# When ScalarE makes the hidden-dimension sine tables of an attention and Fourier-mixing kernel

## The chip, the core and the metric

The kernel runs on one core of a Trainium2 chip. A core has a matrix engine (TensorE, PE in the profile, with its weight loads as PEld), a vector engine (VectorE, DVE), an engine for activation functions (ScalarE, ACT), a general engine (GpSimd, POOL) and a queue engine that mainly issues transfers (SyncE, SP). Each engine works through its own list of instructions in order, and semaphores tie the lists together. DMA engines move data between the chip's memory and the core's on-chip memory; here SP and POOL issue the transfers.

The metric is the time of one execution in microseconds (us). All times below are in us unless another unit stands there.

## What is computed

The reference has two parts, in sequence. Eight batches, 12 heads, 448 tokens, 64 columns a head:

```python
q_n = q / (np.linalg.norm(q, axis=-1, keepdims=True) + 1e-06)
k_n = k / (np.linalg.norm(k, axis=-1, keepdims=True) + 1e-06)
scores = np.matmul(q_n, k_n.transpose(0, 1, 3, 2)) / tau
attn = softmax(scores)                       # written out in the reference
x = np.matmul(attn, v)                       # heads side by side: (8, 448, 768)

X = np.fft.fft(np.fft.fft(x, axis=1), axis=2)
u = x + np.real(X)
un = (u - mean(u)) / np.sqrt(var(u) + 1e-06) # over the 768 columns
out = u + np.maximum(un @ w_ch1, 0.0) @ w_ch2
```

`w_ch1` is 768 x 3072 and `w_ch2` is 3072 x 768.

## The kernel before

**A planner.** The kernel doesn't write its instructions out in order. It adds some 3,000 steps, each with a name, the engines that may do it, a cost for each, a priority, the steps that it depends on and the buffers that it takes (`Plan.add`, L131). `Plan.schedule` (L175) then walks through a modelled time: at each point it takes, for the engine that is free first, the ready step of the lowest priority number, and on ScalarE and VectorE it may wait a little for a more urgent one. The result is one fixed list for each engine; semaphore waits follow from the dependences. `SHIFT` (L32) holds corrections to the priorities of single steps, by name and by how often the name has occurred (`"ldt": {0: 665.9}` adds 665.9 to the first step called `ldt`). A step's name ends in its batch: `ex0_1` is of batch 1.

**Dummy products.** `Plan.fill` (L313) puts groups of six 128-column matmuls, whose result nobody reads, into TensorE's list where the planner sees it idle for at least 0.4 us (L1411 and L1412), one group for each 0.4 us (each 0.7 us in the first 14 us). Behind the first W1 product of batch 0 it does so only where the planner's TensorE is busy for less than three quarters of 3.4 us around. All of them have line L1407 in the profile.

**Tables.** The Fourier transform is done with matmuls against cosine and sine tables. Over the tokens these are `CSs` (and `CSn`, its negative), over the 768 columns `CSd` (and `CSp`, the sines before they are negated). VectorE works out the arguments (L517 to L526) into the space of `U` and `UNT`, which is free at that time. ScalarE takes the sines: step `sins` for `CSs` (L552 and L555), step `sind` for `CSd` and `CSp` (L552 and L554). Then `sinp` (L562) writes `CSp` negated into `CSd`, `half` (L566) halves two rows of `CSs`, and `sinn` (L568) makes `CSn`.

ScalarE evaluates from a loaded set of functions. The set with the sine is loaded ahead of all steps (L357); the step `ldt` (L569) loads the set with Ln and Exp once both sine steps are done, and every Ln and Exp stands behind it. Squares and copies are done under either set.

**One batch's attention.** `first_norm` (L607) is for batches 0 and 1. It loads two halves (g = 0 and 1) of K, Q and the last 64 tokens ("T", of Q and K together): `ld_k0_0`, `ld_q0_0`, `ld_t0_0` and so on, from SP (L651). For each part ScalarE squares it (`sqK0_0`, L658) and VectorE sums the squares by row (`ssK0_0`, L660). K's norms are made together, and those of Q and T together: `ln` (L601) and `nrm` (L603) on ScalarE, which give the root, `eps` (L604) and `rcp` (L605) on VectorE. Then three scalings each for K, Q and T (`scK0_0` to `scT2_0`, L685 and L689, on VectorE or GpSimd), transpositions on TensorE (`tk`, `tq`, `tt`, L713 to L738) and copies out (`ek`, `eq` at L704, `et` at L748, the last into `KTD`). Six pairs of heads follow: score products `qk` (L870 to L883), four exponentials `ex` each (L848, three of 900 columns and one of 450), the product with V `pv` (L901, L907), and division by the sum (`rd`, `x`, L925 and L927).

Later batches use `norm` (L751): seven loads into three staging buffers `STG` (L778), squares `sq` (L787), scaling on GpSimd (L796) and transposition by DMA (L802).

**One batch's Fourier part.** Folds `fa`, `f0`, `f1`, `g` on VectorE (L944 to L973) use the symmetry of the tables; `fs` (L989, L994) multiplies with `CSs`, `te` (L1005, L1006) copies out, `fd` (L1032) multiplies with `CSd` and `CSp`, and `u` (L1060) adds x. Statistics `bs`, `ba` (L1089, L1091), `ln2` and `rs` on ScalarE (L1093, L1095), normalisation `un` (L1098), and the transposition into `UNT`: in batch 0 by TensorE (`tn`, L1108, and copies `eu`, L1116), later by DMA (`tru`, L1119).

**The two big products.** `up` (L1151) multiplies with W1 (`h0_b` to `h23_b`, six matmuls each, L1166) and applies the relu (L1182) on ScalarE or VectorE; the second product is at L1197, in batch 0 as `y`, later as seven products of sums and differences (`m1` to `m7`, twelve matmuls each; here called product sets), with outputs `fin` (L1217, L1229) and GpSimd's addition of u (L1222). Batch 0 has one tile of 128 tokens and a pair of tiles; the "first W1 product" is `h0_0` of the single tile, and `h0_1` that of batch 1. The W1 and W2 loads are issued by GpSimd (L582, L583), as are the V loads (L828 to L831); of the W1 loads the first three wait for one V load. Batch 1's q and k loads wait for the first W1 load.

The attention of the next batch runs among the big products of the batch before, so TensorE has both in one list.

Of the kernel before, what the change touches and what calls it, by code (L numbers as in the profile page):

```python
# [12 lines left out]
B, H, S, DH = 8, 12, 448, 64  # L13
DM = H * DH
# [57 lines left out]
}  # L72

# [342 lines left out]
class Kern:  # L416
# [60 lines left out]
    def consts(self):  # L477
        P = self.P
# [8 lines left out]
        cst = self.cst  # L487
# [980 lines left out]
```

## Time and profile before

| | us |
|---|---|
| time, median of 3 runs | 586.5 |
| lowest and highest | 586.41 and 588.08 |
| the profiled execution's own time | 587.25 |
| its span, first to last instruction | 585.4 |

| engine | busy, us | share of the span |
|---|---|---|
| TensorE | 567.2 | 97% |
| VectorE | 420.0 | 72% |
| ScalarE | 350.0 | 60% |
| GpSimd | 205.8 | 35% |

The profile is of one execution. A timeline row gives start, length, engine, line, operation, output and input tiles with their shapes, how many instructions are merged in the row, and in brackets how long the engine was idle before and what ended that. Instructions that follow each other on an engine overlap a little, so a row's length is somewhat more than its share of the engine's time. A row of waits gives who waited, for whom, how long in total, how often, and the longest. Issues and waits of SP's and POOL's queues are not counted as busy time of those engines. "L" numbers are lines of the kernel before.

### The profile page before, as it was taken

How to read it: one execution, taken by the hardware profiler on the slowest of the kernel's cores; microseconds unless marked ns; L12 is line 12 of the kernel's file. 1: busy time of each engine (PE TensorE's matmuls, PEld its weight loads, DVE VectorE, ACT ScalarE, POOL GpSimd, SP SyncE). 2: the span in 40 equal slices, each digit the busy share in tenths (PEclk: the TensorE clock that was granted, in tenths of full speed). 3: DMA queues.
4: the chain of work that ended last, by engine and by line, in shares of the span. 5: the costliest groups of instructions: out<-in, count | busy, mean ns of one | idle time of the engine just before them, and what ended most of it. 6: DMA issues, size and time to landing. Idle time of an engine off the chain costs nothing.

```text
span 585.4 us, 15046 instructions
## 1 busy us (share of the span) xinstructions
PE 567.2 (97%) x6160; PEld 441.4 (75%) x6160; DVE 420.0 (72%) x980; ACT 350.0 (60%) x672; POOL 205.8 (35%) x316
## 2 busy tenths in 40 slices
PE   3889999999999999999999999999999999999997
PEld 3678887677687776978687688778688688778684
DVE  7879888888688668886778767957777757832222
ACT  7785896259864587548856785356746565224140
POOL 8434424440372524632460346341551200200302
PEclk9999999999999999999999999999999999999999
DMA  9999999972394735944299259472179210130101
GB/s 208 197 231 170 166 182 123 173 168 59 69 165 84 162 70 100 173 105 83 65 141 142 55 149 90 118 166 57 28 127 72 49 49 1 54 82 1 41 16 54
DMA packets 187637, 62.12 MB, mean 106 GB/s; under 512 B 166704, under 2 KB 185392, under 8 KB 187568
## 3 DMA queue, kind: packets, MB, share of 16 engines
q1 hardware_dynamic: 129648, 38.35, 33.8%
q0 software_dynamic: 57920, 22.81, 31.2%
q8 instruction: 48, 0.79, 0.5%
q14 instruction: 21, 0.17, 0.1%
HBM read 51.90 MB, written 11.01 MB: 107 GB/s over the span
## 4 chain that ended last, share of the span: by engine, by line
PE 85%; DMA 5%; DVE 4%; ACT 4%; POOL 1%; issue 1%; SPq 0%; POOLq 0%; DVEq 0%; ACTq 0%
PE PS L1166 34%; PE PS L1197 34%; PE PS L907 5%; PE PS L870 5%; DMA W2b<-in_moe_w_ch_dram 3%; DMA STG<-in_k_dram 2%; PE PS L994 2%; PE PS L901 2%; PE PS L1032 2%; ACT E L848 1%; PE PS L882 1%; PE PS L883 1%; ACT HQ L658 1%; DVE SM L660 0%; DVE ACG L944 0%
## 5 line engine op out<-in xcount | busy, mean ns | idle before, releaser
L1166 PE MATMUL PS<-UNT,W1b 128*128 128x256 bf16 (+1 forms) x2304 | 233.4, 259 | 0.3 <-DVE SM L604 0.3
L1166 PEld LDWEIGHTS PS<-UNT,W1b 128*128 128x128 bf16 x2304 | 199.0, 98 | 23.5 <-issue 2.8
L848 ACT ACTIVATE E<-PS 128x900 bf16<-128x900 f32 (+1 forms) x192 | 147.8, 829 | 28.3 <-PE PS L870 26.0
L1197 PE MATMUL PS<-W2b,HQ 128*128 128x384 bf16 x768 | 134.0, 326 | 0.0
L1182 ACT ACTIVATE HQ<-PS 128x512 bf16<-128x512 f32 x120 | 71.6, 597 | 97.2 <-PE PS L1166 96.6
L796 POOL TENSOR_TENSOR QH<-STG,SM 128x256 bf16<-128x256 f32 x126 | 77.5, 641 | 98.9 <-DVE SM L605 81.1
L1197 PEld LDWEIGHTS PS<-W2b,HQ 128*128 128x128 bf16 x768 | 73.4, 98 | 45.8 <-issue 1.7
L1292 DVE TENSOR_TENSOR HQ<-HQ 128x512 bf16<-128x512 bf16 x141 | 62.6, 460 | 44.5 <-ACT HQ L1182 26.7
L1222 POOL TENSOR_TENSOR OUTB<-OUTB,U 128x192 f32<-128x192 f32 x66 | 38.5, 603 | 147.0 <-ACT OUTB L1217 146.3
L1197 PE MATMUL PS<-TX,HQ 128*128 128x384 bf16 x396 | 71.6, 326 | 0.0
L1197 PEld LDWEIGHTS PS<-TX,HQ 128*128 128x128 bf16 x396 | 37.5, 98 | 23.8 <-issue 1.1
L907 PE MATMUL PS<-VB,E 128*128 128x65 bf16 x1152 | 51.0, 193 | 0.0
L787 ACT ACTIVATE QH<-STG 128x384 f32<-128x384 f32 x84 | 42.4, 521 | 11.7 <-DMA QT<-QH 4.1
L1182 DVE TENSOR_SCALAR HQ<-PS 128x512 bf16<-128x512 f32 x42 | 29.0, 692 | 27.8 <-PE PS L1166 27.7
L907 PEld LDWEIGHTS PS<-VB,E 128*128 128x128 bf16 x1152 | 47.5, 97 | 1.4
L789 DVE TENSOR_REDUCE SM<-QH 128x6 f32<-128x384 f32 x84 | 44.1, 537 | 4.8 <-ACT QH L787 4.6
L901 PE MATMUL PS<-VZ,E 128*128 128x130 bf16 x192 | 41.7, 220 | 0.4 <-ACT E L848 0.4
L1251 POOL DMA_INDIRECT out_dram<-OUTB,IDX x20 | 21.3, 1064 | 57.4 <-DVE OUTB L1229 26.8
L870 PE MATMUL PS<-QT,KT 64*128 64x225 bf16 x576 | 39.1, 259 | 1.1 <-ACT E L848 0.7
L1060 DVE TENSOR_TENSOR U<-ACG,X 128x384 bf16<-128x384 f32 (+3 forms) x70 | 38.3, 575 | 0.8
L1229 DVE TENSOR_TENSOR OUTB<-PS,OUTB 128x384 f32<-128x384 f32 x33 | 18.3, 556 | 23.2 <-PE PS L1197 22.5
L870 PEld LDWEIGHTS PS<-QT,KT 64*128 64x128 bf16 x576 | 22.7, 94 | 15.5 <-issue 5.7
(132 smaller groups left out, 623.6 us busy)
## 6 DMA issues: line engine op xcount, KB each, us to landing
STG<-in_q_dram SPq DMA_DIRECT2D x18, 384.0 KB, 3.9
STG<-in_k_dram SPq DMA_DIRECT2D x18, 384.0 KB, 4.3
VB<-in_v_dram POOLq DMA_DIRECT2D x24, 192.0 KB, 6.7
W1b<-in_moe_w_ch_dram POOLq DMA_DIRECT2D x12, 384.0 KB, 7.2
W2b<-in_moe_w_ch_dram POOLq DMA_DIRECT2D x12, 384.0 KB, 7.6
out_dram<-OUTB SPq DMA_DIRECT2D x7, 384.0 KB
TX<-in_k_dram SPq DMA_DIRECT2D x2, 576.0 KB, 5.8
TX<-in_q_dram SPq DMA_DIRECT2D x2, 576.0 KB, 6.8
```

The lines of the kernel that those rows point to most:

```text
L787: P.add("act", lambda a, sq=sq, src=buf[:, w * x:w * x + w]: a.activation(sq, src, ACTF.Square), t_act(w), pr, f"sq{i}_{b}", reads=bn, wri ...
L789: P.add("dve", lambda v, o=SS[:, i, H // ns * x:H // ns * (x + 1)], sq=sq: v.tensor_reduce(o, sq.rearrange("p (h d) -> p h d", d=DH), AX.X ...
L796: r = v.tensor_tensor(v3(qh)[:, h:h + 4], v3(buf)[:, h:h + 4], RN[:, i, h:h + 4].unsqueeze(2).to_broadcast((128, 4, DH)), AluOp.mult)
L848: return a.activation(o, self.PS[:, bk:bk + nc_, 0:SQ2], ACTF.Exp, scale=1.0 / self.tau)
L870: i = pe.matmul(self.PS[:, bk + h, c0:c0 + NK], self.KT[r, jj, kt * 128:(kt + 1) * 128], self.QT[r, jj, cols], start=True, stop=True)
L901: r = pe.matmul(o, st(6), self.VZ[:, j, :], start=not split, stop=(split and i == 0), skip_group_check=True)
L907: r = pe.matmul(o[:, 65 * h:65 * h + 65], st(2 * kt + h), self.VB[:, kt, 2 * j + h, :], start=(split and i == h == kt == 0), stop=((not sp ...
L1166: r = pe.matmul(self.PS[:, bk, x * n:(x + 1) * n], self.W1b[:, j, ft * 128:(ft + 1) * 128], self.UNT[:, j, cs], start=(j == 0), stop=(j == ...
L1182: return e.activation(o, i, ACTF.Relu) if e is self.nc.scalar else e.tensor_relu(o, i)
L1197: r = pe.matmul(self.PS[:, bk, 0:n], lhs(f), rhs(f), start=(start and f == 0), stop=(stop and f == NF // 2 - 1), skip_group_check=True)
L1222: r = g.tensor_tensor(self.OUTB[:, ob, xs], self.OUTB[:, ob, xs], self.U[:, ut, xs], AluOp.add)
L1292: P.add("dve", lambda v: v.tensor_tensor(cs(o), cs(a), cs(bq), op), 0.46, -0.5, f"{nm}{k}_{b}", reads=rd, writes=hr(o)(k))
```

## The change

Only `CSs` and its sines are made at the start. The load of the Ln and Exp set, now step `ldt0`, stands behind `sins` alone, and batch 0's norms wait for that load. A second load of the sine set (`ldt1`) stands behind all exponentials of batch 0 (`self.exps`); `sind` follows it, and then a load of the Ln and Exp set again (`ldt`), behind which the Ln and Exp steps of batch 1 and of the layer normalisation stand. So ScalarE loads a set four times in all instead of two. `sind` has priority 10 instead of -5.

All corrections in `SHIFT` are replaced; with them the planner gives all five engines other lists.

```diff
 SHIFT = {
-    "iota": {0: -285.2}, "tps": {1: -362.7}, "ktd0": {0: 43.6}, "ix0": {0: -4.2}, "vz1": {1: 15.9}, "half": {0: 121.6}, "ld_k0_0": {0: -761.2},
...
+    "iota": {0: -840.7}, "cst": {0: -19.8}, "tqd": {0: -145.4}, "tps": {0: -28.6, 1: -75}, "vz0": {0: 9.3}, "vz1": {0: 285.2}, "ldt0": {0:
+    230.9}, "sinp": {0: 10.8}, "ldt": {0: 665.9}, "ld_q0_0": {0: 1.8}, "ld_t0_0": {0: 1.8}, "rcp0": {0: -210.2, 1: -210.2}, "sqQ0_0": {0:
...
         def tables():
-            done = [table(sd, self.CSd, DM, -5, "d", [], "CSd")]
-            done.append(table(ss, self.CSs, S, -5, "s", [], "CSs"))
+            ld0 = P.add("act", lambda a: a.preload_act_table_set("natural_log_exp_and_others"), 1.3, -5, "ldt0",
+                        order=[table(ss, self.CSs, S, -5, "s", [], "CSs")])
+            self.trig = trig = P.add("act", lambda a: a.preload_act_table_set("trig_and_small"), 1.3, 10, "ldt1", order=[ld0])
+            done = [table(sd, self.CSd, DM, 10, "d", [trig], "CSd")]
+            self.ldt0 = ld0
...
-            self.ldt = P.add("act", lambda a: a.preload_act_table_set("natural_log_exp_and_others"), 1.3, -5, "ldt", order=done)
+            self.ldt = P.add("act", lambda a: a.preload_act_table_set("natural_log_exp_and_others"), 1.3, 10, "ldt", order=done)
...
         P.add("act", lambda a: a.activation(SS, SS, ACTF.Ln, bias=self.cst[:, 0:1]),
-              0.28, pr, f"ln{b}", reads=ssn + ["cst"], writes=ssn, order=[self.ldt])
+              0.28, pr, f"ln{b}", reads=ssn + ["cst"], writes=ssn, order=[self.ldt if b else self.ldt0])
...
         self.attn(0)
+        self.trig.order += tuple(self.exps)
         for b in range(self.nb):
```

81 rows, old and new, of the table SHIFT are left out of this document.

## The prediction

> **What bounds the kernel now.** I read the page's span, then busy time by stretches cut where the first W1 product of batch 0 starts (53.91), where the first W2 product starts (94.64), and where the last product ends (582.3), and then TensorE's longest wait behind 53.95. In a row of stretches stand its length, then TensorE's busy time, weight loads, VectorE, ScalarE and GpSimd, the granted clock, DMA.
>
> ```profile
> span 585.4 us, 15046 instructions
> ```
> ```profile
> 0.00:53.91 53.91, 40.04 (x587) 32.31 (x588) 45.49 (x102) 40.70 (x67) 28.04 (x53) 1.00 1.27 202
> 53.91:94.64 40.73, 39.59 (x569) 34.12 (x570) 35.14 (x78) 31.79 (x58) 13.21 (x18) 1.00 1.16 170
> 94.64:582.30 487.66, 487.57 (x5006) 374.97 (x5003) 338.81 (x800) 277.47 (x548) 164.54 (x245) 1.00 0.55 90
> 582.30:585.40 3.10, 0.00 (x0) 0.00 (x0) 0.56 (x1) 0.00 (x0) 0.00 (x0) 1.00 0.47 190
> ```
> ```profile
> PE PS L882 <- ACT E L848: 0.8, 1, 0.8
> ```
>
> From 94.64 to 582.30 TensorE is busy 487.57 of 487.66 us at full clock. Between 53.91 and 94.64 it is idle 40.73 - 39.59 = 1.14 us, 0.8 of it the wait of the third fence, for ScalarE. So the span is four terms: the start of the first W1 product (53.91), the matmul work behind it (39.59 + 487.57 = 527.16), the idle time behind it (1.14 + 0.09 = 1.23), and the tail (3.10). They give 585.4. A change in the first 54 us counts only by how far it moves that first product, and each matmul added behind it counts in full.
>
> **The start: what is removed and moved.** ScalarE works alone through a chain there.
>
> ```profile
> 6.37 1.15 ACT L658 ACTIVATE E<-TX 128x1152 f32<-128x1152 f32 x1
> 7.84 0.93 ACT L552 ACTIVATE CS<-UNT,MV 128x770 bf16<-128x770 f32 x1
> 8.67 0.83 ACT L554 ACTIVATE TX<-U 128x770 bf16<-128x770 f32 x1
> 9.51 1.28 ACT L569 ACT_TABLE_LOAD   x1
> 10.81 0.31 ACT L601 ACTIVATE SM<-SM,MV 128x18 f32<-128x18 f32 x1
> 12.74 1.15 ACT L658 ACTIVATE E<-TX 128x1152 f32<-128x1152 f32 x1
> 15.65 0.22 ACT L603 ACTIVATE SM<-SM 128x24 f32<-128x24 f32 x1
> 19.83 2.17 ACT L848 ACTIVATE E<-PS 128x900 bf16<-128x900 f32 x3
> ```
> ```profile
> TX<-in_q_dram SPq DMA_DIRECT2D x2, 576.0 KB, 6.8
> ...
> UNT<-F SPq DMA_TRANSPOSE x25, 2.8
> ```
>
> The square of the first K (6.37) ends at 7.52 in both. Then stood a small square, the two sines that move (7.84 to 9.50) and the table load. In the order built for the changed kernel the load follows at once (7.5 to 8.8), then the square of Q (to 9.9, here it starts at 12.74; its load is now the second that SP issues, at about 1.3, and with 6.8 to landing it is there at 8.1), K's Ln (0.2), the small square (0.4), K's Exp (0.2), a square of the second half (1.05), Q's Ln, a small square, Q's Exp: 12.65. Here that Exp ends at 15.87, so Q's norms come 3.2 us earlier.
>
> VectorE then has more in its way, as it scales K in between:
>
> ```profile
> 11.99 1.50 DVE L689 TENSOR_TENSOR QH<-TX,SM 128x384 bf16<-128x384 f32 x3
> 16.53 0.49 DVE L685 TENSOR_TENSOR TX<-TX,SM 128x128 bf16<-128x128 f32 x2
> 16.94 1.49 DVE L689 TENSOR_TENSOR TX<-TX,SM 128x384 bf16<-128x384 f32 x3
> ```
>
> Its third K scaling (0.5), a reciprocal (0.25), two Q scalings (0.95) and one of the tail (0.25) put the inputs of the first Q transposition at about 15.1, against 17.5 here (16.94 plus one of three): 2.4 us. One of two KTD copies leaves ScalarE, 0.35. I put the first exponential of batch 0 at 17.05, **2.8 us earlier** than 19.83.
>
> ```profile
> 29.27 1.46 ACT L848 ACTIVATE E<-PS 128x900 bf16<-128x900 f32 x2 [0.84 <-PE PS L870]
> 31.21 9.18 ACT L848 ACTIVATE E<-PS 128x900 bf16<-128x900 f32 x12 [0.48 <-PE PS L870]
> 40.27 1.17 ACT L658 ACTIVATE OUTB<-W2b 128x1152 f32<-128x1152 f32 x1
> ```
>
> The 24 exponentials take 20.5 us here, up to the square at 40.27. Twelve take 9.18, so 24 take 18.4, with four small norms some 19.2; the rest is waits (0.84 + 0.48 in these rows) for the second half's scaled rows. Those rows now stand ahead of need by the same kind of count (second-half K scaled from 20.5, last Q at 26, wanted at 26.8). I leave 0.3 of waiting: last exponential at 17.05 + 19.2 + 0.3 = 36.55, **3.8 earlier** (bounds: 2.8 if all waits stay, 4.6 if the rest goes too).
>
> **From the last exponential to the first W1 product.** Here 40.35 to 53.91, 13.55 us.
>
> ```profile
> 41.47 1.35 DVE L660 TENSOR_REDUCE SM<-OUTB 128x18 f32<-128x1152 f32 x1
> 46.81 0.54 ACT L1005 ACTIVATE E<-PS 65x450 bf16<-65x450 f32 x1 [1.38 <-PE PS L994]
> 48.81 1.01 DVE L1060 TENSOR_TENSOR U<-PS,X 128x384 bf16<-128x384 f32 x2
> 49.85 1.02 DVE L1089 BATCH_NORM_STATS2 ACG<-U 128x6 f32<-128x384 bf16 x2
> 53.91 7.53 PE L1166 MATMUL PS<-UNT,W1b 128*128 128x128 bf16 x132 [0.29 <-DVE SM L604]
> ```
>
> ScalarE now gets a load (1.28), the two sines (1.66), and batch 1's square (1.05) first: 4.0 us after the last exponential. VectorE no longer puts the reduction at 41.47 (1.35) ahead of the fold, so the second fold product can run at +4.2; its copy-out ends at +5.8 where it now ends at +7.0 (46.81 + 0.54). The load and the sines hide under fold and product; without that cover they would cost 2.94. That 1.2 us is then given back: VectorE now does five u additions ahead of the statistics instead of two (3 x 0.5), and two K scalings of batch 1 (0.95) ahead of the normalisation. Meanwhile ScalarE does the second table load and two squares and is done at +9.9, before the variance's Ln can start (+10.6). Summed: first W1 product at +13.5, the same. So it starts at **50.05, 3.85 earlier**.
>
> A rule speaks against this change: the Trainium skill (ScalarE: Activation LUTs, What ACT_TABLE_LOAD costs) gives a switch 1.28 us plus a drain of about 1.38, and says to do all of one set before switching. The row at 9.51 shows 1.28, and Ln follows at 10.81, 0.02 behind it; no drain is seen, and the sum goes by the row.
>
> **The negated copies go to GpSimd.** The CSs one (900 columns) stood on VectorE; now it is on GpSimd ahead of the V loads, and the CSd one (770) behind the eighth W1 load.
>
> ```profile
> 5.69 0.74 POOL L530 MEMSET KTD<- 128x768 bf16 x1
> 8.30 0.78 POOL L566 TENSOR_SCALAR CS<-CS 1x225 bf16<-1x225 bf16 x1
> 9.86 3.35 POOL L828 DMA_DIRECT2D VB<-in_v_dram  x3 [0.32 <-POOL IDX L540]
> ```
>
> Not shown by this trace: bounds are 0.74/768 = 0.97 ns a column (0.9 us for 900) and 0.78/225 = 3.5 ns (3.1 us). I take 1.5, nearer the memset, as that row has the same 128 lanes. Starting near 8.9, it lets the V loads go at 10.5 instead of 9.86 (12.1 by the upper bound). SP's loads keep the DMA engines busy to about 13, so I count 0, and 1 at the most. The second lies between +2.9 and at most +5.6, before the product that reads it (+5.9): 0.
>
> **Behind the first W1 product.** The real matmuls are the same. What differs are the groups of six dummy matmuls (L1407): the built order has 11 of them behind the first W1 product, not 2. One stands in batch 1's attention, two before batch 1's first W1 product, eight at the end of batch 1's products. Two of them are seen here:
>
> ```profile
> 186.16 4.06 PE L1197 MATMUL PS<-TX,HQ 128*128 128x384 bf16 x24
> 190.06 4.06 PE L1197 MATMUL PS<-W2b,HQ 128*128 128x384 bf16 x24
> ...
> 256.35 0.83 PE L1407 MATMUL PS<-W1b 128*128 128x128 bf16 x12
> 257.02 1.14 PE L1166 MATMUL PS<-UNT,W1b 128*128 128x256 bf16 x9
> ```
>
> Twelve take 257.02 - 256.35 = 0.67, so a group takes 0.335, and nine more take **3.0 us**. They are nothing only where TensorE would wait anyway, and at the eight it would: the next W1 product's last input is now normalised on VectorE behind an output addition that follows the sixth of seven product sets. A set of twelve takes half of 190.06 - 186.16, 1.95, so six end at 11.7; two VectorE steps of 0.5, a transposition of 2.8 from issue to landing (the page's median for UNT) and a little issue time make some 16, against 13.65 for the seven sets. With the groups TensorE gets there at 16.9 (13.65 + 2.7 and a score product of 0.5), so the time is lost either way and no wait adds to it.
>
> **Idle behind it.** Batch 0's second and third tiles are now transposed after 11 and 15 of the 24 W1 groups; by VectorE's order (0.5 each) their inputs come 0.4 and 0.6 late. Then batch 1's attention, between its first and its last score product:
>
> ```profile
> 64.28:93.78 29.50, 28.48 (x393) 23.35 (x390) 24.46 (x54) 25.34 (x44) 6.69 (x10) 1.00 1.12 176
> ```
> ```profile
> 75.80 0.83 PE L1166 MATMUL PS<-UNT,W1b 128*128 128x256 bf16 x6
> 76.47 0.49 PE L725 MATMUL PS<-TX 128*128 128x128 bf16 x3
> 87.33 0.52 ACT L787 ACTIVATE QH<-STG 128x384 f32<-128x384 f32 x1
> ```
>
> In the built order 19 W1 groups lie in this stretch, not 23. A group takes 76.47 - 75.80 = 0.67, so TensorE has 28.48 - 2.7 = 25.8 to do. ScalarE's four squares of batch 2 (0.52 less overlap, some 1.8; one of them is behind the 0.8 wait) now stand behind the exponentials, copies and output steps about cancel: 25.34 - 1.8 = 23.5. With 3 of this run's 4.2 idle kept it needs 26.5, so TensorE waits 0.7. I take 0.4 + 0.6 + 0.7 and 0.2 more, 1.9, against 1.23 (bounds 0.4 and 4.7).
>
> **Sum**, against the profiled execution: 50.05 + 527.16 + 3.0 + 1.9 + 3.1 = 585.2 of span, 0.2 less than 585.4. That run took 587.25 in all; the median of the runs is 586.5. I carry the difference over: 586.5 - 0.2 = **586.3**.
>
> **Rivals.** (1) *The start's gain survives.* The exponentials lose all waits (first W1 product at 49.3) and the idle time behind is 0.4: 49.3 + 527.16 + 3.0 + 0.4 + 3.1 = 583.0, so 584.1. For: TensorE has only 1.14 idle in that stage now, 0.8 of it for the squares that move. Against: two tile transpositions placed early.
>
> (2) *ScalarE becomes the bound in batch 1's attention.* If its chain keeps the 29.50 us of this run, the four W1 groups that no longer lie between are missed: TensorE waits 29.5 - 25.8 = 3.7, with the two tiles 4.7: 585.2 + 2.8 = 588.0 of span, so 589.1. It decides from the point where ScalarE's chain is longer than 25.8. For: 23.5 of work in 25.8 is 91%, against 86% now. Against: 1.2 of its idle time was the wait for the load of batch 2, which goes.
>
> (3) *Each switch costs twice its row.* If ScalarE lost as much again as a load takes (1.28), the copy-out would slip by 1.1 and the second load would push the variance's Ln 0.75 further: 586.3 + 1.9 = 588.2. Against it stands the 0.02 between load and Ln. The drain of the Trainium skill's section above is this mechanism, and the trace so far speaks against it.
>
> (4) *The change doesn't bring the exponentials forward*, because Q's load lands late: 3.0 + 0.7 more than before, 590.2. Q's 6.8 to landing speaks against.
>
> **How the numbers follow.** A measurement tells 0.3%, 1.8 us, from no change. Forecast 0.47 (585.2 to 587.8 by itself), rival 1 0.24, rival 2 0.21, rival 3 0.04, rival 4 0.04. Faster is rival 1: 0.24. Slower (above 588.3) is rival 2, rival 4 and a part of 3: 0.27. The same is the rest: 0.49. The range goes from 583.5 (rival 1 with the bound of 4.6 on the exponentials) to 589.2 (rival 2).
>
> **What would show it.** First exponential near 17, last near 36.5, first W1 product near 50; both new table loads at 1.28 with the next instruction at once; nine more dummy groups at 0.335 each and no wait beside the last eight. Wrong if the first W1 product is later than 51.5, or if TensorE idles over 3 us behind its first W1 product.

## The result and the profile after

The changed kernel takes 591.02 us, the median of its runs, against 587.33 us for the kernel before beside it; the ratio is 1.0051, with a 95% interval from 1.0034 to 1.0067. It is slower by 0.5%. One of its 20 runs took 1497.18 us, and the ratio leaves it out. The forecast was no change, 586.3 us, and its range ended at 589.2. The profiled execution took 592.52 us in all, 1.5 us more than the median, so its span shows the loss somewhat large.

The page's span, and busy time by stretches of the changed kernel: up to the first W1 product of batch 0 (53.67), up to the first W2 product (96.59), up to the end of the last product (587.00), and the tail. The columns are those of the rows of before.

```profile
span 590.7 us, 15088 instructions
```
```profile
0.00:53.67 53.67, 39.10 (x552) 31.27 (x553) 44.52 (x102) 43.81 (x69) 29.68 (x51) 0.97 1.20 194
53.67:96.59 42.92, 42.92 (x613) 37.91 (x612) 34.53 (x76) 33.17 (x61) 14.97 (x20) 0.96 1.27 169
96.59:587.00 490.41, 488.99 (x5018) 375.96 (x5015) 338.20 (x793) 277.99 (x555) 166.07 (x246) 1.00 0.53 89
587.00:590.70 3.70, 0.00 (x0) 0.00 (x0) 0.56 (x1) 0.00 (x0) 0.40 (x1) 0.83 0.40 159
```

The start, which was to gain 3.85 us, gained 0.24 (53.67 for 53.91). Behind it TensorE is busy 42.92 + 488.99 = 531.91 us and idle 0.00 + 1.42 us. New is the granted clock of 0.97 and 0.96 in the first two rows: before it was 1.00 there. The longest waits of TensorE from 40 us on:

```profile
PE PS L1118 <- DVE F L1108: 2.6, 1, 2.6
PE PS L1176 <- DMA UNT<-F: 0.4, 1, 0.4
PE PS L880 <- DMA KT<-QH: 0.4, 1, 0.4
```

L1118 is the transposition of batch 0's first tile (`tn0_0`), L1108 the tile's normalisation on VectorE (`un0_0`). To see what that waited for, first VectorE's timeline there, then ScalarE's, from its last table load on:

```profile
47.27 0.17 DVE L1101 BATCH_NORM_AGGREGATE MV<-ACG 128x2 f32<-128x12 f32 x1
47.39 1.03 DVE L699 TENSOR_TENSOR QH<-W2b,SM 128x384 bf16<-128x384 f32 x2
50.72 0.67 DVE L1108 TENSOR_SCALAR F<-U,MV 128x768 bf16<-128x768 bf16 x1 [2.31 <-ACT MV L1105]
```
```profile
43.04 1.28 ACT L579 ACT_TABLE_LOAD   x1
44.34 0.31 ACT L611 ACTIVATE SM<-SM,MV 128x18 f32<-128x18 f32 x1
44.92 1.16 ACT L668 ACTIVATE OUTB<-W2b 128x1152 f32<-128x1152 f32 x1 [0.28 <-DVE U L1070]
45.99 0.20 ACT L613 ACTIVATE SM<-SM 128x18 f32<-128x18 f32 x1
49.03 1.16 ACT L668 ACTIVATE W2b<-W2b 128x1152 f32<-128x1152 f32 x1 [2.84 <-DMA W2b<-in_q_dram]
50.10 0.28 ACT L1103 ACTIVATE MV<-MV 128x1 f32<-128x1 f32 x1
50.41 0.20 ACT L1105 ACTIVATE MV<-MV 128x1 f32<-128x1 f32 x1
```

The variance was there at 47.27 + 0.17 = 47.44. Its Ln (L1103) was free to start then, but it stands on ScalarE behind the square of batch 1's first Q half (L668, `sqQ0_1`), and that waited 2.84 us for its load. The load is now the last of the six that SP issues for batch 1; before it was the fourth. It alone, issued at 31.26, in the view of DMA issues (last number: us from issue to landing):

```profile
W2b<-in_q_dram SPq DMA_DIRECT2D x1, 576.0 KB, 17.7
```

So it landed near 49.0, and nothing that the tile needs was in it. While TensorE had no work, its clock fell. Stretches from the last K transposition to the late tile (48.81 to 51.45), to the first W1 product, to the return of the clock (56.96), and on:

```profile
48.81:51.45 2.64, 0.00 (x1) 0.00 (x1) 0.73 (x2) 2.31 (x5) 0.82 (x1) 0.75 1.19 156
51.45:53.67 2.22, 2.22 (x22) 2.22 (x23) 2.12 (x5) 1.25 (x3) 0.82 (x1) 0.50 1.13 139
53.67:56.96 3.29, 3.29 (x33) 3.29 (x32) 2.33 (x6) 0.49 (x1) 0.85 (x2) 0.50 1.36 172
56.96:96.59 39.63, 39.63 (x583) 34.62 (x581) 32.20 (x70) 32.68 (x61) 14.12 (x19) 1.00 1.26 169
```

The clock column (third from the right) is 0.75 in the first row, as the fall comes about half way through it, and then 0.50 until 56.96. The 3.29 us of W1 products in the third row would have taken half as long, so 1.65 us are lost behind the first W1 product, and some more ahead of it. Against the forecast's sum:

| term, us | forecast | profile after |
|---|---|---|
| start of the first W1 product | 50.05 | 53.67 |
| matmul work behind it, dummy groups included | 527.16 + 3.0 | 531.91, of it 1.65 by the halved clock |
| idle behind it | 1.9 | 1.42 |
| tail | 3.1 | 3.70 |
| span | 585.2 | 590.7 |

### The profile page after: what moved, and what is told of

Its sections match the earlier page's. It is cut to its first block, busy times and chain, and to the rows that moved or that the text cites. A ratio compares the mean times of both kernels' runs of the same rounds, so it can differ in the third digit from the quotient of the medians.

```text
span 590.7 us, 15088 instructions
## 1 busy us (share of the span) xinstructions
PE 571.0 (97%) x6178; PEld 445.1 (75%) x6178; DVE 417.8 (71%) x970; ACT 355.0 (60%) x684; POOL 211.1 (36%) x316
## 4 chain that ended last, share of the span: by engine, by line
PE 88%; DMA 5%; POOL 2%; issue 1%; SPq 1%; DVE 1%; ACT 0%; POOLq 0%; DVEq 0%
PE PS L1176 37%; PE PS L1207 33%; PE PS L917 5%; PE PS L880 5%; DMA W2b<-in_q_dram 3%; PE PS L1004 2%; PE PS L911 2%; PE PS L1042 2%; DMA W1b<-in_moe_w_ch_dram 1%; SPq L661 1%; DMA KT<-QH 1%; PE PS L892 1%; PE PS L893 1%; POOL VB L838 1%; PE PS L1418 0%
## 5 line engine op out<-in xcount | busy, mean ns | idle before, releaser
L1176 PE MATMUL PS<-UNT,W1b 128*128 128x256 bf16 (+1 forms) x2304 | 237.3, 260 | 0.4 <-DMA UNT<-F 0.4
L1192 ACT ACTIVATE HQ<-PS 128x512 bf16<-128x512 f32 x122 | 72.8, 597 | 91.0 <-PE PS L1176 89.6
L806 POOL TENSOR_TENSOR QH<-STG,SM 128x256 bf16<-128x256 f32 x126 | 80.5, 664 | 95.4 <-DVE SM L615 81.9
L1207 PE MATMUL PS<-TX,HQ 128*128 128x384 bf16 x396 | 70.4, 326 | 0.0
L1192 DVE TENSOR_SCALAR HQ<-PS 128x512 bf16<-128x512 f32 x40 | 27.6, 691 | 25.9 <-PE PS L1176 25.5
L1227 ACT ACTIVATE OUTB<-PS 128x384 f32<-128x384 f32 x33 | 16.2, 492 | 34.5 <-PE PS L1207 34.3
```

The costliest lines, as they stand in the source:

```text
L806: r = v.tensor_tensor(v3(qh)[:, h:h + 4], v3(buf)[:, h:h + 4], RN[:, i, h:h + 4].unsqueeze(2).to_broadcast((128, 4, DH)), AluOp.mult)
L1176: r = pe.matmul(self.PS[:, bk, x * n:(x + 1) * n], self.W1b[:, j, ft * 128:(ft + 1) * 128], self.UNT[:, j, cs], start=(j == 0), stop=(j == ...
L1192: return e.activation(o, i, ACTF.Relu) if e is self.nc.scalar else e.tensor_relu(o, i)
L1207: r = pe.matmul(self.PS[:, bk, 0:n], lhs(f), rhs(f), start=(start and f == 0), stop=(stop and f == NF // 2 - 1), skip_group_check=True)
```

## The experiments

All act on the planner's finished lists, so nothing else changes its place. `move(engine, step, behind)` takes a step out of an engine's list and puts it behind another (a last number says behind which of several of that name), `hold` puts dummy groups ahead of a TensorE step and `drop` takes some out ahead of one. With these helpers, line numbers are up to 19 higher than in the changed kernel. "First W1" is the first W1 product in the profile; ratios are to the kernel before, run beside each.

| version | first W1 | span | median of runs | ratio, 95% interval |
|---|---|---|---|---|
| the changed kernel | 53.67 | 590.7 | 591.02 | 1.0051 (1.0034 to 1.0067) |
| Q square behind | 50.00 | 584.5 | 587.39 | 0.9996 (0.9977 to 1.0014) |
| wait filled with dummy groups | 52.77 | 586.9 | 588.94 | 1.0028 (1.0013 to 1.0042) |
| changed kernel, no groups behind the first W1 | 55.65 | 593.7 | 592.32 | 1.0076 (1.0054 to 1.0098) |
| Q square behind, no groups behind | 52.97 | 589.3 | 591.16 | 1.0061 (1.0044 to 1.0078) |
| two loads behind the Q load | 50.96 | 586.3 | 588.21 | 1.0011 (0.9997 to 1.0025) |
| Q load second | 51.14 | 585.3 | 589.64 | 1.0034 (1.0016 to 1.0052) |
| both squares behind | 50.15 | 584.6 | 587.58 | 1.0002 (0.9989 to 1.0014) |
| both squares behind, deferral undone | 52.31 | 587.1 | 589.23 | 1.0027 (1.0017 to 1.0037) |
| both behind, earlier tile, four groups | 50.18 | 584.3 | 586.37 | 0.9975 (0.9961 to 0.9989) |
| both behind, earlier tile, all groups | 50.53 | 588.2 | 589.48 | 1.0032 (1.0016 to 1.0048) |
| both behind, four groups | 50.27 | 588.3 | 589.30 | 1.0029 (1.0009 to 1.0048) |
| both behind, earlier tile, four groups, copy-out first | 50.12 | 583.9 | 585.66 | 0.9969 (0.9954 to 0.9983) |
| negated copy behind the V loads | 50.89 | 586.2 | 588.25 | 1.0005 (0.9982 to 1.0028) |

**The square's place.** First the square alone is moved:

```diff
+        self.P.move("act", "sqQ0_1", "ek2_1")
         self.P.emit(self.nc, self.es)
```

> The changed kernel; only the square of batch 1's first Q half (sqQ0_1) moves on ScalarE, from ahead of the variance's Ln of batch 0's first tile to behind the copies of that tile and the third K copy. Theory (ScalarE waits there 2.84 us for the load that lands at 49.01, with the Ln behind it): Ln starts near 47.5 instead of 50.10, the first W1 product near 51.0 instead of 53.67, TensorE's 2.64 us wait ahead of the transposition shrinks below 0.8, its clock stays at 1.00, so the W1 groups behind take 0.335 and not 0.65 each: some 4 us less than the changed kernel's profiled span of 590.7, 586 to 587. Rival (VectorE's five u additions, or the table switches, hold the tile back anyway): first W1 product still past 53, span within 1 us of the changed kernel's.

ScalarE's timeline of that version:

```profile
45.27 0.20 ACT L619 ACTIVATE SM<-SM 128x18 f32<-128x18 f32 x1
47.13 0.29 ACT L1109 ACTIVATE MV<-MV 128x1 f32<-128x1 f32 x1 [1.66 <-DVE MV L1107]
...
50.20 1.18 ACT L674 ACTIVATE W2b<-W2b 128x1152 f32<-128x1152 f32 x1
```

The Ln now waits for the variance alone and starts at 47.13; the first W1 product starts at 50.00, where the forecast had put it (50.05). The clock stayed at 1.00. The span fell by 6.2 us, more than expected, and the runs from 1.0051 to 0.9996. The rival falls. This profiled execution took 586.30 us, 1.1 less than the median, and the changed kernel's 1.5 more than its own, so the spans show more of a gain than the runs.

**A second square in the same place.** The second K half's square (`sqK1_1`) also stands ahead of the Ln. In the version with the Q square behind and no groups, which has the same order ahead of the first W1 product, its load was late instead. ScalarE's rows there:

```profile
45.06 0.31 ACT L617 ACTIVATE SM<-SM,MV 128x18 f32<-128x18 f32 x1
47.49 1.16 ACT L674 ACTIVATE OUTB<-W2b 128x1152 f32<-128x1152 f32 x1 [2.12 <-DVE ACG L1105]
48.56 0.20 ACT L619 ACTIVATE SM<-SM 128x18 f32<-128x18 f32 x1
49.72 0.29 ACT L1109 ACTIVATE MV<-MV 128x1 f32<-128x1 f32 x1 [0.95 <-DVE MV L1107]
```

The wait of 2.12 us is put down to VectorE's statistics (L1105), which this square does not read; its load landed at 47.42 by the trace. The Exp behind it (48.56) holds up a step of the norms on VectorE that stands ahead of the tile's second statistics, so the variance comes late. So both squares were moved, and in two other versions the loads:

```diff
+        self.P.move("act", "sqQ0_1", "ek2_1")
+        self.P.move("act", "sqK1_1", "ek2_1")
```

> The changed kernel; on ScalarE both squares of batch 1's late loads (second K half, first Q half) move behind the copies of batch 0's first tile and the third K copy. Theory: nothing ahead of the variance's Ln depends on a load that lands after 43; first W1 product at 49.5 to 50.3 in every run, clock 1.00, span 583.5 to 585, and the median of the runs about 1 us under that of the version with one square moved, as the K square's wait (2.1 us in one profile) goes too. Rival (the squares are needed soon, and their reductions or the second half's norms then hold batch 1's attention back): waits of 1 us or more on TensorE between 60 and 90.

First W1 product at 50.15, span 584.6, clock 1.00, and no wait of TensorE over 0.4 us behind it. But the median, 587.58, is not under that with one square moved (587.39), so the runs show no gain from the second move.

```diff
+        self.P.move("sp", "ld_q1_1", "ld_q0_1")
+        self.P.move("sp", "ld_t1_1", "ld_q1_1")
```

> The changed kernel; on SyncE alone, batch 1's loads of the second Q half and the second tail (ld_q1_1, ld_t1_1) move behind the load of the first Q half, which so goes from sixth to fourth and the second K half from fifth to third. ScalarE's order is that of the changed kernel. Theory (the Ln waits behind squares for loads): both squares find their data, landed by 41 or so; no wait over 0.8 us on ScalarE ahead of the variance's Ln, first W1 product near 50.0, clock 1.00, span 583.5 to 585.5. Rival (it is the square's place, or the work on VectorE, whatever the load): first W1 product past 52.

With ScalarE's order untouched and the two needed loads earlier, no square waited: Ln at 48.09, first W1 product at 50.96, 2.7 earlier than in the changed kernel. That is later than the 50.0 expected, and the span of 586.3 is 0.8 above what was expected; by ScalarE's timeline the fold product's copy-out, ahead of both squares, ended 0.6 later here (43.24 for 42.61). So the load's lateness is the cause of the wait, not the work around it.

```diff
+        self.P.move("sp", "ld_q0_1", "ld_k0_1")
```

> The changed kernel; on SyncE alone the load of batch 1's first Q half moves from sixth to second, so that the second K half is the last to land (47 to 49 by the landings seen). Theory: the square of that K half, which stands ahead of the Q square on ScalarE, waits in its place, 2 to 4 us, the Ln starts no earlier than 49.3, first W1 product past 52, no gain of over 1.5 us on the changed kernel's profiled span of 590.7. Rival (only the Q load matters): first W1 product near 50, span near 584.5.

Here the theory missed in the profile: the K half's load, now last, had landed by 45.09, when its square was due at 45.36, and the first W1 product started at 51.14. The runs spread from 586.4 to 591.9 us, six of the twelve with a mean granted clock under 0.999, and the median is 589.64. That is as if the wait came in some executions and not in others, but those have no trace, so this run settles nothing.

**The halved clock.** Eight groups of six dummy matmuls are put ahead of `tn0_0`, where TensorE waited:

```diff
+        self.P.hold("tn0_0", 8, self.id_op, warm(self.ID))
```

> The changed kernel with eight more dummy groups on TensorE between the second K transposition of batch 1 and the transposition of batch 0's first tile, where it waited 2.64 us; ScalarE's order is untouched. Theory (the wait itself costs, and beside it the clock that falls to half behind it): ScalarE still waits 2.8 us, the first W1 product starts near 53.3, but the granted clock stays 1.00 and the first W1 groups take 0.335: 1.7 to 2.2 us less than the changed kernel's profiled run. Rival (the clock falls for another reason, as more power drawn by other engines, or is tied to the changed start): clock still 0.5 from about 50 to 57.

ScalarE's row of the waiting square, and TensorE's stretch from 50.20 to 56.80, where the changed kernel had a clock of 0.50:

```profile
47.72 1.16 ACT L687 ACTIVATE W2b<-W2b 128x1152 f32<-128x1152 f32 x1 [1.90 <-DMA W2b<-in_q_dram]
```
```profile
50.20:56.80 6.60, 6.47 (x116) 6.30 (x114) 5.63 (x13) 3.22 (x9) 1.91 (x3) 1.00 1.32 172
```

The square still waited (1.90; the load landed 1.3 earlier than in the changed kernel's profile), and the clock stayed at 1.00. This profile alone doesn't show that the groups kept it there. The tile's normalisation on VectorE and TensorE's rows:

```profile
49.41 0.48 DVE L1127 TENSOR_SCALAR F<-U,MV 128x768 bf16<-128x768 bf16 x1 [1.01 <-ACT MV L1124]
```
```profile
48.63 2.84 PE L1437 MATMUL PS<-TX 128*128 128x128 bf16 x48
51.31 0.50 PE L1137 MATMUL PS<-TX,F 128*128 128x128 bf16 x6
```

The tile was there at 49.89, so without the groups TensorE would have waited some 1.2 us by an estimate (its K transpositions end at 48.79), and a wait of that size can leave the clock at 1.00 (see the versions with the earlier tile below). The eight groups ended only near 51.3, so here they held the product back by 1.4 us; the gain in span, 3.8 for the 1.7 to 2.2 expected, has the earlier landing in it. The runs are better evidence: the mean clock is under 0.999 in one of the 11 with groups, and in ten of the 19 without. And with the Q square behind, it is so in none of the 12 runs that have the groups behind the first W1 product, and in all six of the version without those. So the idle time brings the clock down. In the runs the ratio fell from 1.0051 to 1.0028, and without the wait to 1.0002: some 1.35 us for what the groups saved and 1.5 us for what they didn't, of 587, with intervals about as wide.

**What the deferral is worth.** Both squares moved, and the second sines made at the start again, without the two extra loads:

```diff
+        self.P.order["act"] = [x for x in self.P.order["act"] if x.name not in ("ldt1", "ldt")]
+        self.P.move("act", "sind", "sqK0_0")
```

> As the version with both squares moved, but the second pair of sine tables is made at the start again, ahead of the first of the table loads, and the two other table loads are gone: the deferral is undone, the new priorities stay. Theory as in the prediction (the two switches and the two sines hide behind the last exponential, and at the start they stand in the chain): first exponential 2.1 us later (near 18.4), first W1 product 1.7 to 2.1 us later than with both squares moved, span as much longer. Rival (the deferral only moves the 2.94 us from one end of the chain to the other): first W1 product within 0.5 us.

ScalarE's timeline at the start of this version:

```profile
7.19 0.94 ACT L565 ACTIVATE CS<-UNT,MV 128x770 bf16<-128x770 f32 x1 [0.42 <-DVE UNT L539]
8.04 0.83 ACT L567 ACTIVATE TX<-U 128x770 bf16<-128x770 f32 x1
8.88 1.28 ACT L573 ACT_TABLE_LOAD   x1
...
18.94 0.91 ACT L864 ACTIVATE E<-PS 128x900 bf16<-128x900 f32 x1
```

The first exponential starts at 18.94, against 16.41 with the deferral, and the first W1 product at 52.31 against 50.15; the runs go from 1.0002 to 1.0027. Of 2.53 us at the start 2.16 arrive at the first W1 product, so with these lists the deferral is a gain. The lists were planned with it, though: the kernel before, planned without it, is level with the version with both squares moved (1.0002). What the two switches cost in the end isn't separated here.

**Why the load is late.** GpSimd's timeline of the changed kernel shows the negated copy (L578) ahead of the first V load:

```profile
8.17 2.48 POOL L578 TENSOR_SCALAR HQ<-CS 128x900 bf16<-128x900 bf16 x1
10.72 0.14 POOL L546 IOTA IDX<- 64x8 int32 x1
11.53 1.27 POOL L838 DMA_DIRECT2D VB<-in_v_dram  x1 [0.67 <-POOL IDX L546]
```

```diff
+        self.P.move("pool", "sinn", "ld_v3_0")
```

> The changed kernel; on GpSimd alone the negated copy of 900 columns (2.48 us there in its profile) moves from ahead of batch 0's V loads to behind them, ahead of the W1 loads. Theory (both count: the Q load is last in SyncE's queue, and everything behind the V loads lands later because that copy held them back): the first V load is issued 1.7 us or more earlier than 11.53, the first W1 load lands 1.5 us or more earlier than 24.46, the Q load lands at 46 to 47.5 instead of 49.01, ScalarE's wait shrinks from 2.84 to 0.3 to 1.5 us, the first W1 product starts at 51 to 52.5 and the span is 586 to 588.5. Rival (the order of SyncE's loads alone sets the landing): landing past 48.5, wait over 2.3 us.

The V load went at 8.76, but the copy now stands ahead of the W1 loads, and the first of these landed at 24.77, no earlier than 24.46. The Q load landed at 47.17, the wait was 1.20, first W1 product 50.89 (51 to 52.5 expected), ratio 1.0005. The landing and the wait came as the theory had them, one of its steps did not. And with the same order of loads, the Q load landed between 46.1 and 51.5 in the profiles of twelve of the versions, so this one landing proves little.

That the place in SP's queue counts is shown by the version with the loads reordered, where the Q load was fourth again and landed at 43.49. But in the kernel before, also fourth, it landed at 37.96, 12.3 behind its issue and not 16.0. So the place is not all. The traces show a difference at GpSimd's W1 loads. In the kernel before, the fifth to seventh are issued at 27.74, 31.43 and 32.29, all behind the Q load (25.69). In the changed kernel the fourth to sixth are issued at 26.24, 27.11 and 28.82, all ahead of it (31.26), and none of them had landed by then. Whether these hold the Q load back, no run tests; what GpSimd adds stays open.

**The dummy groups.** The second `fill` is left out:

```diff
-        self.P.fill(first, self.est - 20.0, self.id_op, warm(self.W1b[:, 0, 0:128]), 0.75)
```

> The changed kernel without any dummy group behind the first W1 product (11 fewer: 1 in batch 1's stretch, 2 ahead of batch 1's first W1 product, 8 at the end of its products). Theory as in the prediction (the first three cost 0.335 each, the last eight stand where TensorE waits for a transposition anyway): 1.0 us less, and TensorE idles 2 to 3 us ahead of batch 2's first W1 product; if that idle time halves the clock as the one at 49 did, up to 1.7 us is lost again. Rival (each group costs its 0.335): 3.7 us less and no new wait. The wait at 48.8 to 51.5 stays as it is.

> Both edits together: the square behind the copies and no dummy group behind the first W1 product. Theory: the two gains add, 4 + 1 = 5 us less than the changed kernel's profiled span (585 to 586), so level with or just under the kernel before. Rival (the groups cost their full 3.7): 582 to 583.5, clearly faster than the kernel before.

TensorE's longest waits of the version with the Q square behind and no groups, and the stretches around the first W1 product of batch 2 (199.11):

```profile
PE PS L1182 <- DVE U L1076: 2.3, 1, 2.3
PE PS L886 <- DMA QT<-QH: 1.3, 1, 1.3
```
```profile
195.00:199.20 4.20, 0.65 (x9) 0.45 (x10) 4.10 (x12) 2.69 (x7) 1.53 (x3) 0.94 0.89 207
199.20:203.00 3.80, 3.80 (x23) 2.79 (x23) 1.06 (x3) 1.24 (x4) 2.04 (x3) 0.61 1.11 196
```

Where eight groups stood, TensorE now waits 1.3 + 2.3 us, and the clock falls to half behind it. Without groups neither version is faster than with them (1.0076 for 1.0051, and 1.0061 for 0.9996, six runs each). So those groups stand in a wait, as forecast, and the wait belongs to the new order: batch 2's second tile (`un1_2`) is normalised behind two output additions. Four more versions test that, all with both squares behind. (a) moves this tile ahead, with the Ln of the first tile, the transposition and a score product; (b) drops seven of the eleven groups (the last three lines).

```diff
+        self.P.move("act", "rs0_2", "sq0_4", 0)
+        self.P.move("act", "ln20_2", "sq0_4", 0)
+        self.P.move("sp", "tru1_2", "tru0_2", 0)
+        self.P.move("dve", "un1_2", "ba1_2", 0)
+        self.P.move("dve", "ba1_2", "bs1_2", 1)
+        self.P.move("pe", "qk00_3", "h1_2", 0)
+        self.P.drop("m42_1", 1)
+        self.P.drop("h0_2", 5)
+        self.P.drop("h0_1", 1)
```

> The version with both squares moved, and two more edits. (a) Batch 2's second tile is normalised earlier at the end of batch 1's products: on VectorE ahead of the two output additions, on ScalarE the variance's Ln of the first tile ahead of an output copy, on SyncE its transposition ahead of a Q transposition, on TensorE the first score product of batch 3 behind two W1 groups. (b) Seven of the eleven dummy groups behind the first W1 product go (one of the two ahead of batch 1's first W1 product, six of the eight at the end of its products). Theory (the prediction's: TensorE there waits for this tile's transposition, the groups only fill that wait): the tile is normalised 1.5 to 2 us earlier, batch 2's first W1 product starts 1.8 to 2.4 us earlier after the first W1 product of batch 0 than with both squares moved (145.8 behind it there), span near 582.4, ratio to the kernel before 0.995 to 0.998. Rival (something else, as the third tile or the next scores, holds TensorE in the same place): no gain over 0.5 us, waits of 1.5 us and more.

> Edit (a) alone, all eleven dummy groups kept. Theory: the groups now stand in a wait that is gone, so they cost their 0.335 each: batch 2's first W1 product 145.4 to 146 behind batch 0's, span within 0.7 us of the version with both squares moved. Rival (the earlier tile shortens the stretch by itself): 1 us or more less.

> Edit (b) alone. Theory: TensorE waits where the groups stood, 1.5 to 2 us ahead of batch 2's first W1 product, which starts no more than 0.8 us earlier behind batch 0's; where the idle time brings the clock to half, it is longer than the version with both squares moved by up to 1.5 us. Rival (the groups cost their full time): 2.3 us less, no wait over 0.5 us.

With both, batch 2's first W1 product starts 193.96 - 50.18 = 143.8 us behind batch 0's, 2.0 less than 145.8, and the runs beat the kernel before (0.9975). But the span, 584.3, is only 0.3 less than with both squares moved, not the 582.4 expected: at batch 3's first W1 product 0.3 of the 2.0 is left (207.5 behind batch 0's, for 207.8). With (b) alone TensorE waits in place of the groups and its clock halves, and it is slower (1.0029):

```profile
PE PS L1188 <- DMA UNT<-F: 2.3, 1, 2.3
```
```profile
197.20:200.50 3.30, 3.29 (x16) 2.31 (x17) 0.72 (x2) 0.96 (x3) 1.77 (x3) 0.50 1.11 272
```

With (a) alone the groups stand where nothing is waited for any more. Its span came out 3.5 us longer, not level as expected. By the traces 0.4 of that lies ahead of the first W1 product and 0.9 between it and batch 2's (146.7 instead of 145.8). Up to batch 3's it is 1.65 more, most of it a new wait of 1.31, which the version with (a) and (b) has too; the last 0.6 lies behind. The new wait:

```profile
PE PS L1188 <- ACT HQ L1204: 1.3, 1, 1.3
```

That is a PSUM bank, freed by a W1 copy-out that stands on ScalarE behind two exponentials and a square. The last edit puts it ahead:

```diff
+        self.P.move("act", "relu0_2", "rs2_2")
```

> The version with the earlier tile and four groups, and on ScalarE batch 2's first W1 copy-out (relu0_2) ahead of batch 3's first two exponentials. Theory (there TensorE waits 1.31 us at its third W1 pair for the PSUM bank that this copy-out frees, queued behind the two exponentials): that wait goes, span 1.0 to 1.3 us less than the version without this move (584.3 in its profile), ratio to the kernel before 0.994 to 0.997. Rival (the exponentials, now 0.6 us later, hold the next score products back): the wait turns up ahead of batch 3's scores, no gain over 0.4 us.

TensorE's two longest waits are then these:

```profile
PE PS L892 <- DMA KT<-QH: 1.2, 1, 1.2
PE PS L1188 <- ACT HQ L1204: 0.4, 1, 0.4
```

The wait goes and most of it comes back a little later, ahead of batch 3's scores, as the rival said: 0.4 of span. This version has the lowest time, 585.66 us, ratio 0.9969 (0.9954 to 0.9983), but it is not shown to be faster than the one without this move (0.9961 to 0.9989).

## Why the prediction was wrong

- **The step that failed** is the one from the last exponential to the first W1 product: "ScalarE does the second table load and two squares and is done at +9.9, before the variance's Ln can start (+10.6)". The squares were counted as work, at their durations, and not as waits for data. The second of them waited 2.84 us for a load that landed near 49.0, and was done at 49.03 + 1.16 = 50.19, that is +13.5. The reordered list of SP, which has that load sixth, was at hand, and so was this row of the profile before, for the same kind of load (last number: median us to landing):

```profile
W2b<-in_q_dram SPq DMA_DIRECT2D x2, 576.0 KB, 10.8
```

  Issued last of six, near 31, it was due at 42 by this and at 49 in the run. By 42 it would still have been in time, so the row alone would not have given the wait; as ScalarE was free for the square at 46.19, it would have shown that some four microseconds of delay are enough.
- **What lay behind it** was not in the forecast at all: the wait of 2.64 us ahead of the first W1 product cost the clock too. No rival had either.
- **The steps up to there** held in their sum, in part by luck. ScalarE's timeline, with the first exponential, the last five, the first of the late loads, the sines, and the fold product's copy-out:

```profile
16.34 0.92 ACT L858 ACTIVATE E<-PS 128x900 bf16<-128x900 f32 x1
...
32.86 3.82 ACT L858 ACTIVATE E<-PS 128x450 bf16<-128x450 f32 x5
36.70 1.28 ACT L569 ACT_TABLE_LOAD   x1
37.99 0.94 ACT L559 ACTIVATE CS<-UNT,MV 128x770 bf16<-128x770 f32 x1
...
42.07 0.54 ACT L1015 ACTIVATE E<-PS 65x450 bf16<-65x450 f32 x1 [0.44 <-PE PS L1004]
```

  The first exponential starts at 16.34 (forecast 17.05), the last ends at 36.68 (36.55), the copy-out at 42.61, +5.9 (+5.8), and the variance is there at 47.44, +10.8 (+10.6). But the last exponential came out right by two errors that cancel. The first was 0.7 earlier than forecast (the steps that the forecast lists behind Q's Exp at 12.65 add up to 14.6, where it put 15.1), and the 24 took 20.3, not 19.5: the waits that were to go, down to 0.3, mostly stayed, as 20.3 is nearly the 20.5 of the kernel before.
- **Table loads**: the two late ones took 1.28 each, the next instruction 0.01 and 0.02 behind (37.99 and 44.34). A switch costs its row, and rival 3 falls. The drain of 1.38 us that the Trainium skill gives (ScalarE: Activation LUTs, What ACT_TABLE_LOAD costs) is not seen in either.
- **The negated copy on GpSimd** took 2.48, not 1.5, within the bounds. The V loads went at 11.53, not 10.5; the forecast counted 0 for it, and whether it added to the late landing is open. The second copy ran from +3.1 to +5.3, as forecast.
- **Dummy groups**: eleven behind the first W1 product, as counted. The last eight stand in a wait, and without any of the eleven the time is not less. This step held. What the first W1 product gains, 3.9 in the versions with the squares moved, goes for the most part into these groups and the waits that they fill, so those versions are only level with the kernel before.
- **Idle behind the first W1 product**: 1.42, forecast 1.9. In batch 1's attention TensorE waited for nothing, and in the versions with the squares moved, at a clock of 1.00, it had no idle time between 60 and 97 us either; rival 2 falls.
- **Sum**: with the squares out of the way the first W1 product starts at 50.00 and 50.15 (forecast 50.05), TensorE is busy behind it for 530.35 and 530.43 (530.16) and idle for 0.92 and 0.82 (1.9), the tail is 3.22 and 3.23 (3.1). The span is 584.5 and 584.6, against 585.2, and the runs show 0.9996 and 1.0002. So the sum held but for that wait and the clock behind it.

## What to carry to other kernels

When a scheduler's lists change, read every instruction that now stands ahead of a critical one on its in-order engine, and ask of each not how long it takes but when its data land; a load that moves from fourth to sixth in a queue counts as a change of its own. Filler work is not always a cost: where it stands in a wait, as eight of the eleven groups here, it pays to remove it only together with what is waited for. Where a chain depends on when a load lands, one profile is one draw; put steps that can wait for data behind those that cannot.

## What the runs showed of the hardware

TensorE's clock halved after shorter idle times than a rule says. The Trainium skill (TensorE: Matmul & The Clock Gate, HAM oscillation) asks for no idle gap over about 3.4 us. Here 2.64 us were enough, with the clock at 0.50 from 50.13 to 56.96, and so were 0.51 and 2.32 us with half a microsecond of work between them; a single wait of 1.31 us left it at 1.00. In the five falls that the profiles show ahead of the last product, TensorE had been busy for 0.57 to 1.75 of the 3.41 us ahead of the fall (1.75 in the changed kernel), and the clock then stayed at half for 3.4 or 6.8 us. One stretch with as little work, 1.66 of 3.41 us (47.79 to 51.20 in the version with the Q square behind and no groups), passed without a fall. So not every execution pays it: of the changed kernel's runs, the nine with a mean clock of 0.999 or more average 589.6 us, the ten from 0.993 to 0.997 average 591.9.
